# A gated mix of a long convolution and a dense layer: the signal's second stage on mirrored sums and differences, the taps loaded by pairs onto half of the partitions each

## The chip, the cores and the metric

The kernel runs on one core of a Trainium2 chip. The metric is the device time of one execution in microseconds (us), the median of several runs. The profile is one profiled execution of the same program; its times count from its first instruction.

## The reference

The input u has 2048 rows (time) of 512 channels. Two branches read it, and a gate, one number per row, mixes them. Cut to what matters:

```python
g = sigmoid((u * gate_w).sum(-1, keepdims=True))

# branch A: a state-space convolution, one filter per channel
dt = exp(log_dt)[:, None]
P = exp((dt * A)[:, :, None] * arange(L))          # A, B, C complex, [512, 128]
K = einsum("dn,dnl,dn->dl", C, P, dt * B).real     # the taps, [512, 2048]
a = irfft(rfft(pad(u.T)) * rfft(pad(K)))[:, :L].T + u * Dskip

# branch B: a dense layer, 512 -> 1792 -> 512
b = gelu(u @ w1 + b1) @ w2 + b2

return g * a + (1 - g) * b
```

## The kernel before

All work on TensorE is in float32. The kernel has two parts.

The **front part** (`front`, up to about 398 us) holds three streams of work: the dense branch (`hidden`, `output`; each operand split into a high and a low part, so that every product is three matmuls, lines 917 to 919 and 962 to 964), the taps K (powers of the poles on VectorE and ScalarE, contracted on TensorE at line 726), and the first stage of the transform of both the signal and the taps (`first_stage`, line 438). Every instruction or small group of them is a `Task` with a due time, an estimate of how long it holds its engine, and the tiles it reads and writes. `Plan.run` puts the tasks of each engine in order by due time, among those that are ready, and the instructions are then issued in that order. The due times come from formulas with the constants at the head of the file (`T_0`, `D_EV` and so on).

The transform of 2048 points (with zeros behind it, at shifted frequencies) is cut into two stages. With time as 32 x 64, the first stage transforms the 32 and leaves, for each of 32 frequencies k, 128 rows: real and imaginary parts of 64 slots. It works with products of 32 rows by 64 columns and writes its result to memory: the signal's to `tu_d[k]` (line 459), the taps' to `tk_d[k]` (line 767, eight stores of small pieces for each quarter of the channels). The 64 slots are ordered as 32 and their 32 mirror images (`slot_q`). In `signal` (line 446) a step loads two of sixteen blocks of the input (line 452), runs the first stage on both with the same matrix `c1t`, copies the four results on ScalarE (line 456) and stores them in eight pieces. `early` (line 466) brings 27 of the 32 blocks of `tu_d` back into places that have become free (`attic`, `loft`, `den`).

The **last stage** (`conv`, from about 398 us) is written out by hand. It has 16 loops s, each for two frequencies n = 2s and 2s + 1. Its steps, with the order in which they are issued in a loop:

- `fetch` (line 1129): on SyncE's queue, loads of the taps' blocks `tk_d[k]`, 256 KB on 128 partitions each, into one of eight buffers or, for n from 16 to 23, into the places of `t3`, which hold results only later. For s from 4 on, the five blocks of the signal for which there was no place are loaded as well (line 1274).
- `product(s)`: on VectorE, the complex product of the signal and the taps, six operations (lines 1174 to 1179), into the tiles v.
- `signal(s + 1)`: the second stage of the signal on TensorE, into p2u. `taps(s + 2)`: the same for the taps, into p2k, and two copies on ScalarE (line 1160). Both go through `pair` (line 1146): for the real and the imaginary part c, and for each of the two frequencies, one product of 128 rows by 64 columns. The matrix for c = 0 is f, as loaded; that for c = 1 is f1, made from f by swapping its halves with a sign (`matrices`, line 1131).
- `inverse(s)` (line 1191): the first stage back, into pa, four products of 64 rows by 64 columns.
- `turn(s)`: two copies on ScalarE (line 1197), two stores to `t4_d` (line 1199), and after every eighth frequency the loads of the transposed blocks into `den` and `t3`, mostly on GpSimd's queue.
- after every odd s up to 11, `matrices` makes f1 for the loops s + 3 and s + 4, in two copies of 64 rows on ScalarE (lines 1140 and 1141; for the first two on GpSimd, lines 1137 and 1138). The taps that use it first are those issued in loop s + 1.
- from s = 7 on, `dense` loads the dense branch's results from `out` and `gated` scales them on ScalarE.

Behind the loops, `rest` runs the last products of the dense branch (lines 1245 to 1247) while the last blocks turn, and the last stage back (line 1316) with the gate writes `out`. Before the last stage begins, the front part's last two results are added onto `out` by accumulating stores from the tiles io on GpSimd's queue (line 1006).

Of the kernel before, what the change touches and what calls it, by code (L numbers as in the profile page):

```python
# [9 lines left out]
F32 = mybir.dt.float32  # L10
# [7 lines left out]
P = 128  # L18
L = 2048
D = 512  # L20
# [13 lines left out]
T_0 = 28.031  # L34
T_MLP = 402.005
K_0 = 34.529
T_KG = 347.257
U_0 = 23
U_GAP = 18
LAG = 13.166  # L40
TABLE = 30.571
D_KA = -21.02
D_KP = -70.174
D_S1 = -64.005
D_EV = -0.687
D_H = -44.182
D_LO = -26.872
PS = (2, 3, 1, 2)
N_ACC, N_H, N_PK, N_PU = PS
D_SP = -0.459  # L50
MEM = (6, 2, 3)
N_LD, N_HL, N_ST = MEM
D_XS = -150.061
D_G = 2.936
N_WARM = 13
T_EARLY, T_LOFT, T_DEN = 434.731, 499.385, 583.061
Y_K, Y_U = 40.448, 33.741
W_MLP = (-0.0424, -0.0295, 0.0137)
W_KG = (-0.0358, -0.0266, -0.0229)
W_U = (-0.0255, -0.1355, -0.0209)  # L60
D_MAG = -1.089
D_ROT = 0.621
D_CON = -2.254
D_PHA = 0.57
D_PRE = -1.138
D_XL = 26
D_COE = -4.808
D_OUT = -10.383
D_DTB = -996.723
D_D0A = -269.982  # L70
D_LAST = -1.103
N_REST = 3
D_KA0 = 35
D_DT = 5
D_PRM = -94
D_D0 = 0
D_WAVE0 = -333.922
D_COE0 = -195.511
D_SP1 = -346.272
D_G0 = 14  # L80
D_GW = 568.694
D_XS0 = 115.71
T_PRE = 23
W_CAST = (0, 1, 0, 0, 1, 0, 1, 0, 1, 1, 0, 1, 0, 0)
X_CAST = (1, 1, 1, 1)
D_X0, D_B2, D_B2A, D_DM = -480, 20, -11.213, -79.268
N_G = 9

N_ATTIC, N_LOFT, N_TK = 11, 8, 8
# [5 lines left out]
N_US = N_DEN + N_ROOM  # L95
# [36 lines left out]
def constants():  # L132
# [14 lines left out]
    c1 = np.tile(np.stack([er, ei], 2).reshape(32, 64), (4, 1))  # L147
# [25 lines left out]
    for n, k in enumerate(ko):  # L173
# [5 lines left out]
        g2[n, :, 0, 1] = 1 - 2 * (k1 % 2)  # L179
    f2 = f2.reshape(8, 4, P, 64).transpose(0, 2, 1, 3).reshape(8, P, 256)  # L180
# [130 lines left out]
def gated_mix(  # L311
# [26 lines left out]
    tk_d = dr.tile([32, P, D], F32, name="tk_d")  # L338
# [7 lines left out]
    c1t = cp.tile([P, 64], F32, name="c1t")  # L346

    def places(attic, loft, den):
# [4 lines left out]
    def front(pool, psum, keep, attic, loft, den):  # L353
# [74 lines left out]
        def first_stage(xs, due, evac, ahead=2):  # L428
# [17 lines left out]
        def signal():  # L446
            for s in range(8):
# [3 lines left out]
                for m in range(2):  # L451
                    move(256, lambda m=m, s=s: nc.sync.dma_start(ux[m], xl[2 * s + m]), t - 10, [], [("ux", m)])
# [969 lines left out]
```

## Time and profile before

| | us |
|---|---|
| median of 3 runs (508.15 to 508.41) | 508.25 |
| profiled execution, span from first to last instruction | 506.3 |
| TensorE busy in the span | 494.8 (98%) |
| VectorE busy | 429.0 (85%) |
| ScalarE busy | 347.2 (69%) |
| GpSimd busy | 53.5 (11%) |

The profiled execution's own time is known as its span; 1.95 us lie between it and the median of the runs. In rows of the profile, PE is TensorE's matmuls and PEld its loads of matrices, DVE is VectorE, ACT ScalarE, POOL GpSimd and SP SyncE, which issues most transfers. A float32 product appears as two matmul instructions, so that `pa x8` is the four products of one `inverse`. Matmuls are pipelined: the duration of one is longer than the time from its start to the next one's, and the latter is what a product costs. The transfers of the whole span move 112.32 MB, a mean of 222 GB/s.

### The profile page before, as it was taken

The page shows a single profiled execution, that of the slowest core. Times are in us where ns is not written, and L with a number is a line of the kernel's source. Part 1 is how long each engine was busy: PE and PEld are TensorE (multiplying, and loading weights), DVE is VectorE, ACT ScalarE, POOL GpSimd, SP SyncE. Part 2 cuts the span into 40 slices and gives each one's busy share as a digit, 9 for nine tenths or more (in the row PEclk, how much of TensorE's full clock was granted, in tenths as well). Part 3 has the DMA queues.
Part 4 walks back from the last instruction along what each step waited for, and adds up shares of the span by engine and source line. Part 5 has one row for each costly group of instructions (what it writes and reads, how often), then busy time and mean ns, then how long its engine had stood idle before and what let it go on. Part 6 is the DMA issues. An engine that isn't in the chain of part 4 may idle for free.

```text
span 506.3 us, 12185 instructions
## 1 busy us (share of the span) xinstructions
PE 494.8 (98%) x4798; PEld 380.3 (75%) x4798; DVE 429.0 (85%) x794; ACT 347.2 (69%) x625; POOL 53.5 (11%) x93
## 2 busy tenths in 40 slices
PE   7999999999999999999999999999999999999995
PEld 7886988998889889889789878989889722222551
DVE  6999999998999999999899989999921188877544
ACT  4898757699683889968487997657643445568513
POOL 1001010101002011011110012001010300020003
PEclk9999999999999999999999999999999999999998
DMA  8958896416788545889850276984588997999998
GB/s 288 381 178 235 298 296 219 84 65 200 182 239 222 156 147 126 262 187 238 201 128 2 84 167 156 208 266 104 189 208 180 282 390 266 336 374 382 320 321 312
DMA packets 82680, 112.32 MB, mean 222 GB/s; under 512 B 39644, under 2 KB 41184, under 8 KB 82080
## 3 DMA queue, kind: packets, MB, share of 16 engines
q1 hardware_dynamic: 74704, 87.06, 53.7%
q0 software_dynamic: 7264, 21.73, 18.3%
q10 hardware_dynamic: 656, 2.75, 1.7%
q8 instruction: 38, 0.62, 0.5%
q14 instruction: 18, 0.15, 0.1%
HBM read 61.71 MB, written 49.81 MB: 220 GB/s over the span
## 4 chain that ended last, share of the span: by engine, by line
PE 70%; DVE 13%; DMA 7%; ACT 4%; SPq 2%; issue 2%; DVEq 0%; ACTq 0%
PE pk L726 10%; PE acc L962 7%; PE ph L917 7%; PE ph L919 7%; PE ph L918 7%; PE acc L964 7%; PE acc L963 6%; PE p2u L1152 5%; PE p2k L1152 4%; PE pa L1191 3%; PE pb L1316 3%; DMA tk<-tk_d 2%; PE ph L438 2%; DVE y L689 2%; SPq L767 2%
## 5 line engine op out<-in xcount | busy, mean ns | idle before, releaser
L917 PE MATMUL ph<-xh,wh 128*128 128x256 f32 x448 | 127.7, 285 | 2.2 <-ACT wh L826 1.6
L919 PE MATMUL ph<-xh,wl 128*128 128x256 f32 x448 | 127.1, 284 | 0.4 <-DVE wl L828 0.4
L918 PE MATMUL ph<-xlo,wh 128*128 128x256 f32 x448 | 126.7, 283 | 0.0
L917 PEld LDWEIGHTS ph<-xh,wh 128*128 128x128 f32 x448 | 85.2, 190 | 9.5 <-issue 5.0
L918 PEld LDWEIGHTS ph<-xlo,wh 128*128 128x128 f32 x448 | 85.1, 190 | 1.8
L919 PEld LDWEIGHTS ph<-xh,wl 128*128 128x128 f32 x448 | 85.1, 190 | 1.0 <-DVE wl L828 1.0
L962 PE MATMUL acc<-wh,hh 128*128 128x512 f32 x206 | 83.2, 404 | 0.1
L964 PE MATMUL acc<-wh,hl 128*128 128x512 f32 x206 | 80.9, 393 | 0.5 <-DVE hl L947 0.5
L963 PE MATMUL acc<-wl,hh 128*128 128x512 f32 x206 | 80.9, 393 | 0.0
L934 ACT ACTIVATE ph<-ph,b1t 128x256 f32<-128x256 f32 x112 | 50.4, 450 | 43.6 <-PE ph L919 41.8
L726 PE MATMUL pk<-y,den 128*32 128x64 f32 x2048 | 61.4, 290 | 0.0
L726 PEld LDWEIGHTS pk<-y,den 128*32 128x32 f32 x2048 | 57.2, 136 | 3.5 <-issue 1.4
L962 PEld LDWEIGHTS acc<-wh,hh 128*128 128x128 f32 x206 | 38.7, 188 | 17.8 <-issue 7.4
L947 DVE TENSOR_TENSOR hl<-ph,hh 128x512 fp32r<-128x512 f32 (+1 forms) x62 | 38.4, 620 | 14.9 <-ACT hh L937 14.6
L689 DVE TENSOR_TENSOR y<-y,ea 128x64 f32<-128x64 f32 (+4 forms) x80 | 45.5, 569 | 2.1 <-ACT y L679 1.5
L964 PEld LDWEIGHTS acc<-wh,hl 128*128 128x128 f32 x206 | 38.7, 188 | 10.3 <-DVE hl L947 1.7
L963 PEld LDWEIGHTS acc<-wl,hh 128*128 128x128 f32 x206 | 38.7, 188 | 6.2
L937 ACT CAST hh<-ph 128x512 fp32r<-128x512 f32 (+1 forms) x62 | 33.0, 533 | 9.4 <-PE acc L963 6.2
L532 DVE TENSOR_TENSOR loft<-den,zz 128x256 f32<-128x256 f32 (+2 forms) x48 | 37.4, 779 | 0.7
L533 DVE TENSOR_TENSOR loft<-den,zz 128x256 f32<-128x256 f32 (+2 forms) x48 | 37.3, 777 | 0.0
L701 DVE TENSOR_TENSOR y<-y,loft 128x2048 f32<-128x2048 f32 x16 | 36.6, 2288 | 0.6 <-ACT loft L650 0.5
L1160 ACT COPY k<-p2k 128x512 f32<-128x512 f32 x32 | 18.5, 585 | 23.8 <-PE p2k L1152 8.0
(190 smaller groups left out, 876.0 us busy)
## 6 DMA issues: line engine op xcount, KB each, us to landing
tu_d<-attic SPq DMA_DIRECT2D x64, 128.0 KB, 3.9
tk_d<-sk SPq DMA_DIRECT2D x32, 256.0 KB, 5.3
t_d<-sa SPq DMA_DIRECT2D x32, 256.0 KB, 5.4
tk<-tk_d SPq DMA_DIRECT2D x24, 256.0 KB, 5.1
attic<-in_xt_dram SPq DMA_DIRECT2D x16, 256.0 KB, 5.1
xh_d<-xh SPq DMA_DIRECT2D x8, 512.0 KB, 5.0
xl_d<-xlo SPq DMA_DIRECT2D x8, 512.0 KB, 4.6
attic<-in_xs_dram SPq DMA_DIRECT2D x16, 256.0 KB, 4.9
```

Of the source, the lines that this page charges most:

```text
L532: vec(2 * m, lambda: vv.tensor_mul(t, a, br), due, [ka, *kb], [kt])
L689: nc.vector.tensor_mul(both(n, 64 - 3 * n, n), both(0, 64 - n, n), an)
L726: nc.tensor.matmul(pks[q][32 * j : 32 * j + 32, :, gg], x[:, r, :, ch], y[:, r, :, ch], start=(r == 0), stop=(r == 1), skip_group_check=True,)
L917: nc.tensor.matmul(p, h, xh[xk][:, d], start=(d == 0), stop=False)
L918: nc.tensor.matmul(p, h, xlo[xk][:, d], start=False, stop=False)
L919: nc.tensor.matmul(p, lo, xh[xk][:, d], start=False, stop=(d == 3))
L934: nc.scalar.activation(phs[q][:, n], phs[q][:, n], AF.Gelu_apprx_tanh, bias=b1t[:, f : f + 1])
L947: nc.vector.tensor_sub(lo, phs[q][:, 0:nf], hi.bitcast(F32))
L962: nc.tensor.matmul(a, h, wh[1][w], start=start, stop=False)
L963: nc.tensor.matmul(a, h, wl[1][w], start=False, stop=False)
L964: nc.tensor.matmul(a, l, wh[1][w], start=False, stop=(j == 3))
L1152: nc.tensor.matmul(out[64 * i : 64 * i + 64], w, x, start=True, stop=True)
```

## The change

**The signal.** A step of `signal` now takes block s and its mirror image, block 8 + s. It loads one into each buffer, negates the second on ScalarE, and adds the other block onto each with an accumulating load on GpSimd's queue, so that the buffers hold the sum and the difference. The first stage runs on both, on the difference with the real and imaginary columns of the matrix swapped. The 64 rows of each part of `tu_d[k]` are then 32 of sums and 32 of differences, and in the second stage the real part needs only the first 64 rows and the imaginary part only the last 64: each product has 64 rows in place of 128, and f alone, without f1.

**The taps.** `tk_d` is split in two halves of the slots, and `fetch` brings the blocks of a pair of frequencies into one tile, with one load for partitions 0 to 63 and one for 64 to 127. The order of the rows of f follows, and `matrices` makes f1 in four pieces of 32 rows in place of two of 64. The eight buffers of one block become five of two.

**Places.** Five more places (`shed`) let `early` bring all 32 blocks of the signal, so the five loads in the last stage go.

**Order.** Every task of the front part gets a due time from a list `DUE`, and the constants at the head are changed. The scratch space for descriptors of GpSimd's transfers is set to 2048.

```diff
-T_0 = 28.031
-T_MLP = 402.005
+T_0 = 30.181
+T_MLP = 394.707
...
+D_UL, D_UN, D_UA = -26.734, -19.978, -26.418
...
-N_ATTIC, N_LOFT, N_TK = 11, 8, 8
+N_ATTIC, N_LOFT, N_TK = 11, 8, 5
...
-N_US = N_DEN + N_ROOM
+
+DUE = (
+    -14012, -3058, -1619, -990, 254, -1062, 252, 2164, -206, -437, -438, -558, -1021, -1047, -3081, -2791, -3683,
...
+)
...
-    c1 = np.tile(np.stack([er, ei], 2).reshape(32, 64), (4, 1))
+    c1 = np.concatenate([np.stack(z, 2).reshape(32, 64) for z in ((er, ei), (ei, er))], 1)
+    c1 = np.tile(c1, (4, 1))
...
+    f2 = f2.reshape(32, 2, 2, 32, 64).transpose(0, 2, 1, 3, 4)
     f2 = f2.reshape(8, 4, P, 64).transpose(0, 2, 1, 3).reshape(8, P, 256)
...
-    tk_d = dr.tile([32, P, D], F32, name="tk_d")
+    tk_d = dr.tile([2, 32, 64, D], F32, name="tk_d")
...
-        return [den[:, k] for k in range(N_DEN)] + rooms + rooms[: 32 - N_US]
+        return [den[:, k] for k in range(N_DEN)] + rooms + [shed[:, k] for k in range(32 - N_DEN - N_ROOM)]
...
-                        nc.tensor.matmul(bank[64 * m : 64 * m + 64], c1t[rs], x[rs], start=True, stop=True)
+                        w = c1t[rs, 64 * m * mirrored : 64 * m * mirrored + 64]
+                        nc.tensor.matmul(bank[64 * m : 64 * m + 64], w, x[rs], start=True, stop=True)
...
                 for m in range(2):
-                    move(256, lambda m=m, s=s: nc.sync.dma_start(ux[m], xl[2 * s + m]), t - 10, [], [("ux", m)])
+                    move(256, lambda m=m, s=s: nc.sync.dma_start(ux[m], xl[8 * m + s]), t + D_UL, [], [("ux", m)])
+                act(512, lambda: nc.scalar.mul(ux[1], ux[1], -1.0), t + D_UN, [], [("ux", 1)])
+                for m in range(2):
+                    move(
+                        540, lambda m=m, s=s: nc.gpsimd.dma_start(ux[m], xl[8 * (1 - m) + s], accum_op=ALU.add),
+                        t + D_UA, [], [("ux", m)], queue="GP", hold=0.8,
+                    )
...
-                            128, lambda m=m: nc.sync.dma_start(rows[:, 8 * s + 4 * m + r], st[k][64 * m : 64 * m + 64]),
-                            t, [("st", k)], [("u_d", 8 * s + 4 * m + r)], out=True,
+                            128, lambda m=m: nc.sync.dma_start(rows[:, 32 * m + 4 * s + r], st[k][64 * m : 64 * m + 64]),
+                            t, [("st", k)], [("u_d", 32 * m + 4 * s + r)], out=True,
...
-                first_stage(xs, t, evac)
+                first_stage(xs, t, evac, mirrored=1)
...
-            for n in range(N_US):
+            for n in range(32):
...
+                sr = slice(h // 2 % 2 * 16, h // 2 % 2 * 16 + 16)
...
-                        tk_d[:, :, d : d + 64].rearrange("k (c s) g -> (k c) s g", c=2)[:, ss],
+                        tk_d[h // 4, :, :, d : d + 64].rearrange("k (c s) g -> (k c) s g", c=2)[:, sr],
...
+        for t, due in zip(pl.tasks, DUE, strict=True):
+            t.due = due / 10
         for t in pl.run():
             t.fn()
...
-        def fetch(n):
-            if 16 <= n < 24:
-                t2s[n] = t3[:, n]
+        def fetch(s):
+
+            n = 2 * s
+            if 8 <= s < 12:
+                t = t3[:, n : n + 2]
             else:
-                t2s[n] = pool.tile([P, D], F32, tag="tk", name=f"tk{n}", bufs=N_TK)
-            nc.sync.dma_start(t2s[n], tk_d[ko[n]])
+                t = pool.tile([P, 2, D], F32, tag="tk", name=f"tk{s}", bufs=N_TK)
+            t2s[n], t2s[n + 1] = t[:, 0], t[:, 1]
+            for h in range(2):
+                rows = tk_d[h].rearrange("(a b) q d -> b q a d", b=8)[ko[n] % 8][:, ko[n] // 8 : ko[n] // 8 + 2]
+                nc.sync.dma_start(t[64 * h : 64 * h + 64], rows)
...
-            if m < 2:
-                nc.gpsimd.tensor_scalar(f1[0:64], f[64:128], -1.0, None, ALU.mult)
-                nc.gpsimd.tensor_copy(f1[64:128], f[0:64])
-            else:
-                nc.scalar.mul(f1[0:64], f[64:128], -1.0)
-                nc.scalar.copy(f1[64:128], f[0:64])
+            for a in (0, 64):
+                re, im = slice(a, a + 32), slice(a + 32, a + 64)
+                if m < 2:
+                    nc.gpsimd.tensor_scalar(f1[re], f[im], -1.0, None, ALU.mult)
+                    nc.gpsimd.tensor_copy(f1[im], f[re])
+                else:
+                    nc.scalar.mul(f1[re], f[im], -1.0)
+                    nc.scalar.copy(f1[im], f[re])
...
-                w = mats[n // 4][0][c][:, n % 4]
-                x = t2s[n] if r else us[n]
+                if r:
+                    w, x = mats[n // 4][0][c][:, n % 4], t2s[n]
+                else:
+                    h = slice(64 * c, 64 * c + 64)
+                    w, x = mats[n // 4][0][0][h, n % 4], us[n][h]
                 nc.tensor.matmul(out[64 * i : 64 * i + 64], w, x, start=True, stop=True)
...
-            for n in range(2 * s + N_ROOM, min(2 * s + N_ROOM + 2, 32)) if s > 3 else ():
-                nc.sync.dma_start(us[n], tu_d[ko[n]])
...
+    shed = keep.tile([P, 32 - N_DEN - N_ROOM, D], F32, name="shed")
...
-    nc = bacc.Bacc("TRN2", target_bir_lowering=False, num_devices=1)
+    nc = bacc.Bacc("TRN2", target_bir_lowering=False, num_devices=1, dynamic_dma_scratch_size=2048)
```

More of the change, by code (lines that the diff above doesn't have):

```diff
@@ L33 @@
 NB = 2 * NSB
-T_0 = 28.031
-T_MLP = 402.005
[L36 to L47, printed above, removed]
+T_0 = 30.181
+T_MLP = 394.707
+K_0 = 37.105
+T_KG = 355.412
+U_0 = 22.335
+U_GAP = 18.311
+LAG = 13.918
+TABLE = 32.374
+D_KA = -25.837
+D_KP = -7.351
+D_S1 = -39.706
+D_EV = -4.468
+D_H = -49.631
+D_LO = -47.233
 PS = (2, 3, 1, 2)
 N_ACC, N_H, N_PK, N_PU = PS
-D_SP = -0.459
+D_SP = 6.17
+D_UL, D_UN, D_UA = -26.734, -19.978, -26.418
 MEM = (6, 2, 3)
 N_LD, N_HL, N_ST = MEM
-D_XS = -150.061
+D_XS = -73.683
 D_G = 2.936
 N_WARM = 13
[L56 to L61, printed above, removed]
-D_ROT = 0.621
[L63 to L71, printed above, removed]
-N_REST = 3
[L73 to L84, printed above, removed]
+T_EARLY, T_LOFT, T_DEN = 268.769, 88.647, 688.804
+Y_K, Y_U = 39.373, 32.963
+W_MLP = (-0.0402, -0.0382, 0.0137)
+W_KG = (-0.0552, -0.0303, -0.0248)
+W_U = (-0.0299, -0.1355, -0.0182)
+D_MAG = -1.108
+D_ROT = 0.621
+D_CON = -2.853
+D_PHA = 0.521
+D_PRE = -0.43
+D_XL = -21.252
+D_COE = -12.806
+D_OUT = -43.76
+D_DTB = -1371.399
+D_D0A = -89.28
+D_LAST = 3.23
+N_REST = 3
+D_KA0 = 66.334
+D_DT = 3.379
+D_PRM = -94.216
+D_D0 = 19.524
+D_WAVE0 = -640.267
+D_COE0 = -98.47
+D_SP1 = -328.657
+D_G0 = -7.172
+D_GW = 807.205
+D_XS0 = 238.814
+T_PRE = 62.946
+W_CAST = (0, 0, 0, 1, 1, 0, 1, 0, 0, 1, 0, 1, 0, 0)
 X_CAST = (1, 1, 1, 1)
-D_X0, D_B2, D_B2A, D_DM = -480, 20, -11.213, -79.268
+D_X0, D_B2, D_B2A, D_DM = -252.638, 6.525, -2.867, 78.983
 N_G = 9
-N_ATTIC, N_LOFT, N_TK = 11, 8, 8
+N_ATTIC, N_LOFT, N_TK = 11, 8, 5
 ASIDE = (4, 6, 13, 14)
@@ L345, in gated_mix, with places, front @@
     gate = cp.tile([P, 2, 16], F32, name="gate")
-    c1t = cp.tile([P, 64], F32, name="c1t")
-    def places(attic, loft, den):
+    c1t = cp.tile([P, 128], F32, name="c1t")
+    def places(attic, loft, den, shed):
         rooms = [attic[:, k] for k in range(N_ATTIC)] + [loft[:, k * D : k * D + D] for k in range(N_LOFT)]
-        return [den[:, k] for k in range(N_DEN)] + rooms + rooms[: 32 - N_US]
-    def front(pool, psum, keep, attic, loft, den):
+        return [den[:, k] for k in range(N_DEN)] + rooms + [shed[:, k] for k in range(32 - N_DEN - N_ROOM)]
+    def front(pool, psum, keep, attic, loft, den, shed):
         pl = Plan()
@@ L426, in front, with first_stage @@
         step = [0]
-        def first_stage(xs, due, evac, ahead=2):
+        def first_stage(xs, due, evac, ahead=2, mirrored=0):
             q = (step[0] + ahead) % N_H
@@ L1107, in front, with conv @@
         return sorted(late, key=lambda e: e[0])
-    def conv(pool, ps, late, attic, loft, den):
+    def conv(pool, ps, late, attic, loft, den, shed):
         sas = [pool.tile([P, D], F32, name=f"sa{k}", bufs=1) for k in range(6)]
         zs = [pool.tile([P, D], F32, name=f"z{k}", bufs=1) for k in range(2)]
-        us = places(attic, loft, den)
+        us = places(attic, loft, den, shed)
         ko = k0_order()
@@ L1349, in gated_mix @@
     ):
-        late = front(kp, ps, keep, attic, loft, den)
+        late = front(kp, ps, keep, attic, loft, den, shed)
     with (
@@ L1354, in gated_mix @@
     ):
-        conv(fp, ps_f, late, attic, loft, den)
+        conv(fp, ps_f, late, attic, loft, den, shed)
 _NAMES = [
```

20 lines of the change are left out of this document (10 added, 10 removed), and 87 rows, old and new, of the table DUE.

## The prediction

> **What bounds the kernel now.** I read the page first, then the busy time by stretch, then the chain of work that ended last, then the timeline of one loop of the last stage, then the transfers.
>
> ```profile
> PE 494.8 (98%) x4798; PEld 380.3 (75%) x4798; DVE 429.0 (85%) x794; ACT 347.2 (69%) x625; POOL 53.5 (11%) x93
> PE 70%; DVE 13%; DMA 7%; ACT 4%; SPq 2%; issue 2%; DVEq 0%; ACTq 0%
> ```
>
> TensorE is busy for 98% of the span and holds 70% of the chain. The average hides stages, so the next view cuts the span into stretches (us; then for each engine busy us and instructions; granted clock, DMA share, GB/s).
>
> ```profile
> 0.00:20.00 20.00, 17.00 (x110) 15.74 (x111) 15.66 (x39) 11.50 (x24) 2.08 (x10) 1.00 0.90 322
> 20.00:60.00 40.00, 38.35 (x262) 32.62 (x261) 38.90 (x90) 37.12 (x67) 2.95 (x4) 1.00 0.78 249
> 60.00:240.00 180.00, 180.00 (x2116) 157.30 (x2118) 175.10 (x329) 140.80 (x254) 17.34 (x30) 1.00 0.69 189
> 240.00:300.00 60.00, 59.42 (x736) 50.53 (x728) 57.00 (x108) 46.22 (x83) 7.40 (x14) 1.00 0.48 120
> 300.00:398.00 98.00, 98.00 (x1085) 86.61 (x1084) 70.25 (x117) 57.10 (x101) 11.13 (x19) 1.00 0.74 189
> 434.00:472.00 38.00, 38.00 (x200) 10.43 (x196) 29.90 (x49) 25.98 (x49) 3.67 (x7) 1.00 1.01 375
> 394.00:506.00 112.00, 106.00 (x542) 41.53 (x541) 72.75 (x116) 56.98 (x104) 14.78 (x21) 0.99 0.95 333
> ```
>
> The planned front part (up to about 398 us) leaves TensorE idle for only 3.00 + 1.65 + 0.58 = 5.2 us, most of that at the start. From 394 us the transfers are busy for 95% of the time, and for all of it between 434 and 472 us: whatever shortens the last stage pushes against that.
>
> The chain (start, us, what) shows what a loop of the last stage costs: pa is the inverse, p2u the signal's second stage, p2k the taps'.
>
> ```profile
> 408.91 1.69 PE pa L1191 x8
> ...
> 414.18 1.02 PE pa L1191 x8
> ...
> 432.59 1.02 PE pa L1191 x8
> 433.61 1.87 PE p2u L1152 x8
> 435.48 1.72 PE p2k L1152 x8
> 437.19 1.02 PE pa L1191 x8
> ...
> 469.42 1.02 PE pa L1191 x8
> ...
> 475.60 1.02 PE pa L1191 x8
> ```
>
> One loop takes 437.19 - 432.59 = 4.60 us and is TensorE from end to end. The inverses run from 408.91 (loop 0) over 414.18 (loop 1) and 469.42 (loop 13) to 475.60 us (loop 15).
>
> **The change, part by part.** *The signal's products.* The timeline of one loop (start, duration, engine, line; in brackets what the engine waited for):
>
> ```profile
> 432.52 1.09 PE L1191 MATMUL pa<-v,cc 64*64 64x512 f32 x8
> 433.54 1.08 PE L1152 MATMUL p2u<-attic,cc 128*64 128x512 f32 x4
> 433.67 1.07 ACT L1197 COPY sa<-pa 128x512 f32<-128x512 f32 x2 [0.37 <-PE pa L1191]
> 434.45 1.03 PE L1152 MATMUL p2u<-attic,f 128*64 128x512 f32 x4
> 434.77 0.41 ACT L1140 ACTIVATE f<-cc 64x256 f32<-64x256 f32 x1
> 435.19 0.40 ACT L1141 COPY f<-cc 64x256 f32<-64x256 f32 x1
> 435.31 1.03 PE L1152 MATMUL p2k<-t,cc 128*64 128x512 f32 x4
> 435.74 0.14 PEld L1152 LDWEIGHTS p2k<-t,f 128*64 128x64 f32 x2 [0.29 <-ACT f L1141]
> 436.16 1.03 PE L1152 MATMUL p2k<-t,f 128*64 128x512 f32 x4
> 437.12 1.09 PE L1191 MATMUL pa<-v,cc 64*64 64x512 f32 x8
> ```
>
> From start to start: pa 1.02, p2u 0.91 and 0.86, p2k 0.85 and 0.96 us, together 4.60. A p2u block is two products of 128 rows, one per half of the output columns. After the change each product has 64 rows, and the four of a loop fall on four different quarters of the array, as the four of pa do now; pa does its four in 1.02 us. So p2u's 0.91 + 0.86 = 1.77 us become one block: at least 0.86 (a block with no change of shape near it), at most pa's 1.02. I take 0.91, because pa and p2u would now have one shape and the change of shape moves behind p2u, to p2k, without a new one. The loop then needs 4.60 - 1.77 + 0.91 = 3.74 us of TensorE (3.69 to 3.85).
>
> The Trainium skill's page TensorEngine Tiling (Array Packing), section Key Properties, says that a change of tiling mode drains the array. The trace agrees: the blocks that stand at a change of shape are the long ones (1.02, 0.91 and 0.96 against 0.86); by that rule alone the block is 0.86 and the loop 3.69 us.
>
> *Is VectorE next?* In loop 0, behind the wait at L1175, it ran without a break:
>
> ```profile
> 403.72 0.69 DVE L1174 TENSOR_TENSOR v<-p2u,k 128x512 f32<-128x512 f32 x1 [4.05 <-ACT k L1160]
> 406.37 0.69 DVE L1175 TENSOR_TENSOR v<-p2u,k 128x512 f32<-128x512 f32 x1 [1.95 <-DMA out_dram<-io]
> ...
> 409.37 0.69 DVE L1174 TENSOR_TENSOR v<-p2u,k 128x512 f32<-128x512 f32 x1
> ```
>
> L1175 to the next L1174 are five operations in 3.00 us: 0.60 each, so the six of a loop make 3.60 us, just under 3.74. VectorE doesn't bind, by 0.14 us.
>
> *The matrices f1: the wait that replaces what is saved.* ScalarE now makes f1 in two copies of 64 rows; after the change in four of 32 rows, each with the same 256 elements per row, so 0.42 and 0.40 us twice. They stand on ScalarE behind the copies of pa, and the taps of the very next loop need them for their second block. Now they are done at 435.59 and the block starts at 436.16, so nothing is lost. After the change they are done 0.82 us later, 3.89 us after the start of the inverse; with the 0.15 us to the weight load and its 0.14, the block starts at 4.18. TensorE would be there at 1.02 + 0.91 + 0.86 = 2.79. So TensorE waits 1.39 us in each loop that follows matrices: behind loops 1, 3, 5, 7, 9 and 11. Such a pair of loops takes 4.18 + 0.96 + 3.74 = 8.88 us against 9.20 now: 0.32 us saved instead of 1.72. Queued behind the copies on ScalarE are the next two copies of p2k; TensorE needs their banks only a loop later, so they cost nothing more. Six pairs from loop 1 to loop 13: **-1.9 us**. For m 0 and 1 GpSimd makes the four pieces, twice as long as now; there the first products wait for a transfer until 406.37 us, which covers it: 0.
>
> *Loop 0 and its start.* The first product waits for the two accumulating stores out_dram<-io: L1175 starts when the second has landed. That is a wait for memory: v[1] lies where io lay. The tap tiles grow from 8 x 2 to 5 x 4 KB per partition, which by the order of the allocations moves v by 4 KB, so that L1174 falls on that same wait. It then starts at 406.37 and one more operation stands behind it: +0.6 us (bounds: +0.6; or -2.0, the L1175 wait, if no tile lies there any more). From loop 0 to loop 1 the 5.27 us lose p2u's 0.86: together **-0.3 us**.
>
> *Loops 13 to 15* take 6.18 us. There are no taps any more, and TensorE will run into VectorE: the product of loop 14 begins some 1.5 us ahead of the inverse of loop 13 (the taps' 0.86 + 0.96 lie between, less the way from engine to engine), two products take 7.2 us, and 0.3 lead back to TensorE: 6.0 us, **-0.2 us**. Behind that, the tail (the outputs held back, the last stage, the stores) is unchanged and shifts as a whole: 0.
>
> *The signal's first stage* (front part). Eight more negations on ScalarE and sixteen accumulating transfers on GpSimd's queue; the products keep their number, and only their matrices differ. The nearest rows:
>
> ```profile
> L456 ACT COPY attic<-pu 128x512 f32<-128x512 f32 x16 | 9.6, 598 | 6.9 <-DMA tu_d<-attic 6.8
> out_dram<-b2b POOLq DMA_DIRECT2D x16, 256.0 KB, 5.9
> xh<-xh_d POOLq DMA_DIRECT2D x8, 512.0 KB, 4.2
> ```
>
> Eight times 0.6 us is 4.8 us on an engine that is idle for over a fifth of the front part, and 5.9 us more from load to product, eight times in 300 us. Behind the transfers on GpSimd's queue stand the reloads of xh, which TensorE does need. I cost it at 0, as the plan places it early; were the cover gone, TensorE would wait some 6 us a step.
>
> *The new order of the front part* (a due time for each task) issues the same products. It can win at most the idle time behind the first 20 us, 1.65 + 0.58 = 2.2 us; for a loss the nearest row is a reload of xh that comes late by its whole 4.2 us. I take 0, and -2.2 to +4.2 for the range.
>
> *The rows of the taps.* The same 32 x 256 KB, but each load on 64 partitions, and five loads of the signal move from the last stage to the front part. What a transfer on 64 partitions costs is seen at the stores of the signal's first stage, when they run alone, beside transfers on all partitions:
>
> ```profile
> 250.00:250.40 0.40, 0.40 (x4) 0.32 (x3) 0.40 (x1) 0.04 (x1) 0.00 (x0) 1.00 1.00 215
> 410.00:414.00 4.00, 4.00 (x22) 1.06 (x16) 4.00 (x8) 1.64 (x3) 0.00 (x0) 1.00 1.05 388
> ```
>
> Fully busy engines carry 215 GB/s on one half and 388 on all. So a load of 0.67 us could take up to 1.22. Between 394 and 506 us the engines work 0.95 x 112 = 106.4 us; five loads fewer make 103.0. The forecast's end (503.9) leaves 109.9 - 1.6 (the end, where the last stores trickle) = 108.3, so the loads may cost 5.3 us more, 0.16 each, before they set the end. With other transfers and the other half queued beside them I expect them under that: two halves in flight at once would carry twice 215.
>
> **Sum.** -1.9 - 0.3 - 0.2 = -2.4 us: span 506.3 to 503.9. The median of the runs is 508.25, so 1.95 us lie around the span, which I leave: **505.9 us**.
>
> **The rivals.** *ScalarE's copies don't hold TensorE* (say that they shrink with the rows): then each of the 12 loops gains 0.86, 10.3 us in place of 1.9: 508.25 - 10.3 - 0.3 - 0.2 = 497.4. Against it: a copy of 64 rows already takes 0.40. Chance 0.10.
>
> *The half-partition loads set the end* (slower). One mechanism: engines that meet on one half carry 215 GB/s. From 0.16 us more per load it eats the gain, from 0.23 us (7.4 us in all) the kernel is slower than now; at the full 0.55 it is 103.0 + 17.6 = 120.6 us from 394 on, a span of 514.6 and a time of 516.5. For it: the 215 row, and a last stage already at 0.95. Against it: the taps run five pairs ahead. Chance 0.14, a part of it mild. The Trainium skill, SBUF — State Buffer, section "Can I just issue two DMAs to hit both halves?", says no: two halves serialize. By it the full price is paid, 516.5. The 215 row agrees for a half alone; no row here shows two loads into both halves.
>
> *The front part moves*, by its new order or by the accumulating transfers: 0.08 faster (505.9 - 2.2 = 503.7), 0.08 slower (505.9 + 4.2 = 510.1).
>
> *It cancels*: a little from the loads, a little from the start, within 0.2% (1 us, which is about what a measurement of this kernel can tell from none): chance 0.12.
>
> The forecast itself, faster by 1 to 5 us, has 0.48. **Chances:** faster 0.48 + 0.10 + 0.08 = 0.66; same 0.12; slower 0.14 + 0.08 = 0.22. **Range:** 498.5 to 510.5; it leaves out the first rival (0.10) and the full price of the second (some 0.10).
>
> **What would show it.** Right: in the chain p2u x8 at about 0.9 us; in every second loop ScalarE's f1 as releaser of the weight load of p2k, over 1 us; inverses of a pair 8.9 us apart, single ones 3.7; L1174 of loop 0 waiting for out_dram<-io. Wrong: p2k or pa waiting for tk<-tk_d (the loads), pairs 7.5 us apart (no wait for f1), p2u x8 still at 1.7 (the quarters don't run together), or a last stage that starts more than 2 us off 398 (the order).

## The result and the profile after

The changed kernel takes 522.13 us (median of 4 runs, 521.45 to 523.92) against 508.2 for the kernel before: a ratio of 1.0285 [1.025, 1.032]. It is slower by 14 us, outside the range given. The profiled execution has a span of 519.3 us, 13.0 more than before. Where the median and the ratio of a run below don't match, some of its executions took longer at a lower granted clock; the ratio leaves these out.

The first lines of the page, of the changed kernel (busy time by engine; shares of the chain that ended last):

```profile
PE 489.5 (94%) x4798; PEld 376.5 (73%) x4798; DVE 429.9 (83%) x793; ACT 357.8 (69%) x647; POOL 70.1 (14%) x113
PE 67%; DMA 15%; issue 5%; ACT 4%; SPq 4%; DVE 3%; POOL 1%; ACTq 1%; DVEq 0%; POOLq 0%
```

TensorE is busy for 5.3 us less, in a span that is 13.0 longer; transfers hold 15% of the chain where they held 7%. The stretches of the changed kernel (us; busy us and instructions of PE, PEld, DVE, ACT, POOL; granted clock, DMA share, GB/s):

```profile
20.00:60.00 40.00, 36.82 (x253) 31.30 (x251) 37.56 (x87) 32.98 (x59) 5.00 (x7) 1.00 0.87 249
60.00:240.00 180.00, 177.45 (x2003) 153.45 (x1996) 174.06 (x327) 144.36 (x260) 24.52 (x38) 1.00 0.74 200
406.00:410.00 4.00, 0.00 (x0) 0.00 (x0) 0.04 (x1) 0.00 (x0) 1.04 (x2) 0.65 1.09 265
414.00:430.00 16.00, 14.99 (x94) 3.81 (x96) 14.47 (x24) 9.22 (x18) 0.27 (x1) 1.00 1.06 230
```

In the front part TensorE idles 3.18 us from 20 to 60 us (1.65 before) and 2.55 from 60 to 240 (none before), and the clock granted in the first 20 us is 0.91: from 8 to 12 us it is 0.59, by which these 4 us lose some 1.6 (an estimate). Against the kernel before that makes some 5 of the 6.4 us that the front part ends later. The rest was not found. Between 406 and 410 us TensorE does nothing at all. From 414 to 430 us the transfer engines are busy throughout and carry 230 GB/s.

Four rows of the timeline cut the span into parts. Of the kernel before: the last product of the front part, the first of the taps, the inverses of loops 0 and 15.

```profile
398.03 0.28 PE L919 MATMUL ph<-xh,wl 128*128 128x256 f32 x1
398.24 0.64 PE L1152 MATMUL p2k<-tk,cc 128*64 128x512 f32 x1
408.91 0.64 PE L1191 MATMUL pa<-v,cc 64*64 64x512 f32 x1 [0.93 <-DVE v L1178]
475.53 0.66 PE L1191 MATMUL pa<-v,cc 64*64 64x512 f32 x4
```

The same four of the changed kernel:

```profile
404.39 0.28 PE L1020 MATMUL ph<-xh,wl 128*128 128x256 f32 x1
410.66 1.12 PE L1265 MATMUL p2k<-tk,cc 128*64 128x512 f32 x2 [5.99 <-DMA tk<-tk_d]
419.96 0.66 PE L1304 MATMUL pa<-v,cc 64*64 64x512 f32 x4
486.89 0.64 PE L1304 MATMUL pa<-v,cc 64*64 64x512 f32 x1
```

| part of the span, us | before | after | difference |
|---|---|---|---|
| to the last product of the front part | 398.0 | 404.4 | +6.4 |
| from there to the first product of the taps | 0.2 | 6.3 | +6.1 |
| to the inverse of loop 0 | 10.7 | 9.3 | -1.4 |
| to the inverse of loop 15 | 66.6 | 66.9 | +0.3 |
| to the end | 30.8 | 32.4 | +1.6 |

So the time is lost ahead of the last stage (6.4), at its start (6.1), and inside it, where nothing is gained although its loops have less to do. The chain of the changed kernel shows why the last two go together (L1251 is a copy of `matrices`):

```profile
402.78 9.94 DMA tk<-tk_d
412.74 8.29 DMA tk<-tk_d
421.04 8.40 DMA t<-tk_d
429.51 7.03 DMA t_d<-sa
...
438.49 0.41 ACT f L1251
438.95 1.98 PE p2k L1265 x4
```

For 34 us the end hangs on tap loads, one behind the other in SyncE's queue, and then on a store of the inverse's result that stands behind them. ScalarE can't copy the next result until that store has landed, f1 stands behind that copy, and the taps' second block behind f1. Beyond 451 us the loops run free, and there they look as forecast:

```profile
451.50 1.02 PE pa L1304 x8
452.53 0.86 PE p2u L1265 x8
453.38 1.87 PE p2k L1265 x8
455.25 1.02 PE pa L1304 x8
...
459.15 1.08 PE p2k L1265 x4
460.23 1.02 PE pa L1304 x8
```

A single loop takes 3.75 us (451.50 to 455.25), the loop behind matrices 4.98, a pair 8.73.

### The profile page after: what moved, and what is told of

The parts are those of the page before. It is cut to its first block, busy times and chain, and to the rows that moved or that the text cites. A ratio compares the mean times of both kernels' runs of the same rounds, so it can differ in the third digit from the quotient of the medians.

```text
span 519.3 us, 12259 instructions
## 1 busy us (share of the span) xinstructions
PE 489.5 (94%) x4798; PEld 376.5 (73%) x4798; DVE 429.9 (83%) x793; ACT 357.8 (69%) x647; POOL 70.1 (14%) x113
## 4 chain that ended last, share of the span: by engine, by line
PE 67%; DMA 15%; issue 5%; ACT 4%; SPq 4%; DVE 3%; POOL 1%; ACTq 1%; DVEq 0%; POOLq 0%
PE pk L826 10%; PE ph L1018 8%; PE ph L1019 8%; PE acc L1063 8%; PE ph L1020 8%; PE acc L1064 7%; PE acc L1065 7%; DMA ux<-in_xl_dram 4%; DMA tk<-tk_d 4%; PE p2k L1265 3%; PE ph L532 3%; PE pa L1304 2%; DMA t_d<-sa 2%; SPq L868 2%; PE p2u L1265 2%
## 5 line engine op out<-in xcount | busy, mean ns | idle before, releaser
L1018 PE MATMUL ph<-xh,wh 128*128 128x256 f32 x448 | 129.1, 288 | 3.5 <-ACT wh L927 2.9
L826 PE MATMUL pk<-y,den 128*32 128x64 f32 x2048 | 61.6, 291 | 0.8 <-DVE y L812 0.8
```

Source lines behind the costliest of these rows:

```text
L826: nc.tensor.matmul(pks[q][32 * j : 32 * j + 32, :, gg], x[:, r, :, ch], y[:, r, :, ch], start=(r == 0), stop=(r == 1), skip_group_check=True,)
L1018: nc.tensor.matmul(p, h, xh[xk][:, d], start=(d == 0), stop=False)
```

## The experiments

The theory after the result: three independent costs, the halves of the taps, the four pieces of f1, and the front part; the rivals are named with each run. Each kernel was timed beside the kernel before on the same chip; the kernel before had medians from 506.6 to 508.2 there, so ratios are compared rather than times of different calls.

### The loads by themselves: m1_loads_alone

Behind the end of the kernel before, six groups of loads of tk_d, one after another.

```diff
+        done()
+        for load in (
+            whole, lambda: alternating((nc.sync, nc.sync)), one_half, every_second,
+            lambda: alternating((nc.sync, nc.scalar)), whole,
+        ):
+            load()
+            done()
```

> The kernel before, with loads from tk_d into t3 added behind its end, in six groups that wait for one another: 12 whole loads of 256 KB; 12 of 256 KB on partitions 0-63 and 64-127 in turn, as the change has them; 12 of 128 KB on partitions 0-63 alone; 12 of 256 KB on every second partition; the halves in turn again, one half from SyncE's queue and the other from ScalarE's; 12 whole ones again. Theory (two halves in one queue run one behind the other, each at half the rate): 0.67 us a load whole, 1.14 for the halves in turn (as the changed kernel's trace has them), 0.57 for the 128 KB, 0.67 for every second partition. Rival (the loads were slow because of what ran beside them): 0.67 in all groups of 256 KB.

Three stretches: whole loads, halves in turn from one queue, loads of every second partition.

```profile
504.00:512.00 8.00, 0.00 (x0) 0.00 (x0) 0.00 (x0) 0.00 (x0) 0.00 (x0) 0.50 1.00 358
520.00:528.00 8.00, 0.00 (x0) 0.00 (x0) 0.00 (x0) 0.00 (x0) 0.00 (x0) 0.50 1.07 225
548.00:552.00 4.00, 0.00 (x0) 0.00 (x0) 0.00 (x0) 0.00 (x0) 0.00 (x0) 0.50 1.02 373
```

The last two columns decide: the engines are equally busy, and with halves they carry 225 GB/s against 358 and 373. Whole loads land mostly 0.64 to 0.68 us apart, halves of the same 256 KB 1.13 to 1.19, so a load costs some 0.5 us more, with nothing else in flight. The Trainium skill, SBUF — State Buffer, section "Can I just issue two DMAs to hit both halves?", says that two such transfers serialize; the 225 agrees, the 334 of e4 below doesn't. Every second partition at the full rate shows that it is the half that costs, not the 64 partitions. Halves issued in turn from two queues landed 0.97 us apart on average (0.55 to 1.74), so that a part of the loss stays. The loads of 128 KB on one half landed 0.67 us apart (0.57 was expected), about as fast as they were issued, one every 0.64 us.

### The taps whole again: e1_whole_taps

```diff
-            for h in range(2):
-                rows = tk_d[h].rearrange("(a b) q d -> b q a d", b=8)[ko[n] % 8][:, ko[n] // 8 : ko[n] // 8 + 2]
-                nc.sync.dma_start(t[64 * h : 64 * h + 64], rows)
+            for i in range(2):
+                nc.sync.dma_start(t[:, i], tk_d[ko[n + i]])
```

The signal gets a copy of f in its own row order, in wider constants.

> The changed kernel with the taps stored and loaded as before, on all 128 partitions (two loads of 256 KB per pair, four tiles of two in place of five); the signal's products get a copy of the matrix in their own order of rows, 1 MB more of constants in all; f1 stays in four pieces, the order of the front part stays. Theory (the half loads cost what lies behind the front part's end): the front part ends at 404.5 us as in the changed kernel, the first inverse comes 10.7 us later (415.2, in place of 420.0), and loops 0 to 13 take some 57 us in place of 61.5: span near 509, time near 511. Rival (the loads are hidden, the front part and cold clocks make the rest): at least 518.

515.44 us, ratio 1.0152 [1.0118, 1.0187]: 6.7 us below the changed kernel, half of the loss. Its front part and the start of its last stage:

```profile
403.47 0.28 PE L1020 MATMUL ph<-xh,wl 128*128 128x256 f32 x1
408.52 1.08 PE L1265 MATMUL p2k<-tk,cc 128*64 128x512 f32 x1 [4.77 <-DMA tk<-tk_d]
418.67 0.66 PE L1304 MATMUL pa<-v,cc 64*64 64x512 f32 x4
480.28 0.64 PE L1304 MATMUL pa<-v,cc 64*64 64x512 f32 x1
```

Loop 0 to 15 takes 61.6 us in place of 66.9, so 5.3 of the 6.7 lay in the loops: in the changed kernel the inverses at 432.42 and 446.46, a pair of loops, lie 14.0 us apart, in e1 every such pair 8.7. The front part and the 5 us to the first taps stay: these are not the halves. The theory had expected the start of the last stage to come back as well, and so a time near 511.

### The order of before: e2_old_order and e3_whole_old_order

Both drop the list `DUE` and take the constants of the kernel before; e3 has whole taps as well, so that only the signal's part of the change is left.

> The changed kernel with the constants at its head as before and without the list of due times; the three new constants of the signal's loads stay. Half loads stay. Theory (the new order costs the front part its 6.3 us): the front part ends at 398 to 400 us again and the time is 516 to 518. Rival (the accumulating loads and the negations cost it): the front part still ends at 403 to 406 and the time stays at 521 to 524.

> The changed kernel with the front part in the order of the kernel before (its constants, no list of due times) and the taps loaded whole, 256 KB on 128 partitions each: of the change, only the signal is left (sums and differences by accumulating loads, half-height products, all 32 blocks fetched early, f1 in four pieces). Theory (the accumulating loads delay TensorE in the front part, whatever the order): the front part's last product is as late as with the old order and half loads (406.9, against 398.0 before), the loops run at 3.75 and 4.98, and the time is about 515. Rival (the half loads were what made the front part late in the old order too): last front product at 398 to 400, time 505 to 507.

e2 takes 516.69 us (1.0184 [1.0156, 1.0211]), e3 513.39 (1.0115 [1.0088, 1.0142]). Of e3:

```profile
404.99 0.28 PE L929 MATMUL ph<-xh,wl 128*128 128x256 f32 x1
405.20 0.64 PE L1172 MATMUL p2k<-tk,cc 128*64 128x512 f32 x1
```

In e2 the front part ends at 406.97: the time that its theory named was met, the reason for it was not. Two things follow. The front part is as late in the order of the kernel before, so the signal's part brings it along; and the wait at the start of the last stage is gone, so that one belongs to the new order. The traces point at how. The two accumulating stores of io and the first tap loads, in the changed kernel, then in e3:

```profile
399.03 1.72 POOL L1107 DMA_DIRECT2D out_dram<-io  x2 [1.10 <-ACT io L1084]
400.62 0.61 SPq L1237 DMA_DIRECT2D tk<-tk_d  x1
```

```profile
399.04 0.84 SPq L1143 DMA_DIRECT2D tk<-tk_d  x2
402.84 1.72 POOL L1016 DMA_DIRECT2D out_dram<-io  x2
```

Issued behind the stores, the first load took 9.1 us to land in the changed kernel, 8.6 in e1 and 7.3 in e15 (below), and landed 0.2 to 0.5 us after the second store; issued ahead of them, it took 4.3 us in the kernel before, 5.6 in e3 and 4.5 in e17. No run moved these two stores alone, so their part is argued from the traces. The halves cost 3.3 us in this order (e2 against e3).

### The halves in the kernel before: e4_halves_alone and e11_halves_old_layout

e4 is the kernel before with the pair loads by halves out of the undivided tk_d; e11 is e1 with the same loads.

```diff
+            rows = tk_d.rearrange("(a b) q d -> b q a d", b=8)[ko[n] % 8][:, ko[n] // 8 : ko[n] // 8 + 2]
+            for h in (slice(0, 64), slice(64, 128)):
+                nc.sync.dma_start(t[h], rows[h])
```

> The kernel before, with the rows of the taps loaded by pairs onto half of the partitions each (256 KB, the same bytes and number of loads, four tiles of two in place of eight of one); nothing else of the change. Theory (half loads run at half the rate and hold the start of the last stage): the first inverse comes 6 to 10 us later than 408.9 and none of it is won back, so 514 to 518. Rival (the loads are hidden behind the loops): 508 to 509.

> The kernel of e1_whole_taps with the taps loaded by pairs onto half of the partitions each, but out of the undivided tk_d of the kernel before, as in e4_halves_alone: it differs from the changed kernel in where the rows lie in memory, not in which partitions they go to. Theory (two halves in turn move at the rate of one, wherever they come from): landings 1.1 us apart between 412 and 430, packets of 2 KB at about 150 ns, time 520 to 523, as the changed kernel. Rival (the divided layout is what makes the halves slow, and out of the undivided one they overlap, as the 0.8 us and 102 ns of e4_halves_alone hint): landings 0.8 apart, time 516 to 518.

e4 took only 508.79 us, ratio 1.0045 [1.0025, 1.0066]: the price named for it was missed. A stretch of e4:

```profile
412.00:420.00 8.00, 8.00 (x46) 2.12 (x44) 7.41 (x13) 5.03 (x10) 0.00 (x0) 1.00 1.05 334
```

The engines carry 334 GB/s here, a packet of 2 KB takes 102 ns on average, and the loads land about 0.8 us apart; in the changed kernel it is 230 GB/s, 149 ns and 1.14 us. So in this run halves did overlap in part. e11 has e4's layout and the changed kernel's order, and its loads are 1.05 apart; it takes 519.89 us (1.0237 [1.0186, 1.0288]), 0.85% more than e1 by the ratios. So the halves are slow out of e4's layout too. What decides whether two halves overlap, the phase in which the engines meet or what else is in flight, stays open.

### What costs in the front part: e5, e8, e9, e10, e6

Five runs take the signal's first stage apart; the code is cut to the calls that change. e5: the second loads without the accumulation. e8: negations and second loads left out, all else at its place. e9: no change but one due time in the kernel before. e10: sixteen more loads, which nobody waits for, in the kernel before, with the change's scratch space for descriptors. e6: sums on GpSimd.

```diff
e5  -  nc.gpsimd.dma_start(ux[m], xl[8 * (1 - m) + s], accum_op=ALU.add)
    +  nc.gpsimd.dma_start(ux[m], xl[8 * (1 - m) + s])
e8  -  nc.scalar.mul(ux[1], ux[1], -1.0)
    +  None
    -  nc.gpsimd.dma_start(ux[m], xl[8 * (1 - m) + s], accum_op=ALU.add)
    +  None
e9  -  nc.sync.dma_start(ux[m], xl[2 * s + m]), t - 10,
    +  nc.sync.dma_start(ux[m], xl[2 * s + m]), t - 26.734,
e10 +  nc.gpsimd.dma_start(shed[:, 2 * (s % 2) + m], xl[2 * s + m])
e6  +  nc.gpsimd.tensor_add(ux[0], ux[0], ux[1])
    +  nc.scalar.mul(ux[1], ux[1], -2.0)
    +  nc.gpsimd.tensor_add(ux[1], ux[1], ux[0])
```

> The kernel of e3_whole_old_order with the sixteen accumulating loads of the signal made plain loads of the same blocks, same queue, same tasks, same order. Left out: the sums and differences, so the signal's transform is of wrong data. Theory (what costs is the accumulation itself, whose packets take 176 ns per 2 KB against 84): the front part's last product comes back to 399 to 401 and the time to about 508. Rival (what costs is the longer chain of load, negation, second load, product and the place of these steps in ScalarE's and GpSimd's order): last front product within 2 us of that of e3_whole_old_order, time within 2 us of it.

> The kernel of e3_whole_old_order with the eight negations and the sixteen second loads of the signal left out, while every other step stays at its place in the order of every engine. Left out: the sums and differences, so the signal's transform is of wrong data. Theory (TensorE waits because a step of the signal now has three steps more in a row, load, negation, second load, before its product): the front part's last product comes back from 404.9 to 398 to 400 us, and the time from 513.4 to about 507. Rival (it is the order of the other steps, which the added ones have upset, not the added work): last front product at 403 to 406, time at 512 to 514.

> The kernel before with one constant of the order changed: the signal's loads are due 26.734 us ahead of their step, as in the changed kernel, in place of 10. No work is added. Theory (the front part's order is so finely set that a step moved for no other reason costs several us): last front product at 402 to 406 against 398.0, time 512 to 515. Rival (the order holds such a shift): last front product within 1 us of 398, time within 1 us of the kernel before.

> The kernel before with sixteen more loads of the signal's blocks, issued on GpSimd's queue right behind the loads that stand there, into places that nobody reads, and with the scratch space for descriptors of GpSimd's transfers at 2048 as in the change. The order of everything else is as before. Theory (4 MB more of transfers in the front part, a half of it in its first 100 us, where the transfer engines are busy for 61 to 94%, delays the loads that TensorE waits for): last front product at 400 to 402, time 510 to 512. Rival (the bytes cost nothing, the chain or the order does): last front product within 0.7 us of 398.0, time within 1 us of the kernel before.

> The kernel of e3_whole_old_order with the sums and differences made on GpSimd: both blocks loaded plainly as before, a sum in place (1.27 us for 128x512 in the profile), ScalarE's multiplication by -2, a second sum in place. No accumulating loads for the signal. Theory (the accumulating loads make the front part late): last front product at 399 to 401, time about 508. Rival (the longer chain and its place in the order do, whatever makes the sums): last front product over 404, time over 512.

The last product of the front part in e8, then in e9, each from its timeline:

```profile
403.89 0.28 PE L929 MATMUL ph<-xh,wl 128*128 128x256 f32 x1
```

```profile
402.64 0.28 PE L919 MATMUL ph<-xh,wl 128*128 128x256 f32 x1
```

Against the 398.03 of the kernel before, and with the same row of the other runs:

| run | time, us | ratio | front part against before |
|---|---|---|---|
| e3, the signal's part | 513.39 | 1.0115 [1.0088, 1.0142] | +7.0 |
| e5, no accumulation | 513.08 | 1.0111 [1.0081, 1.0141] | +7.4 |
| e8, added steps left out | 511.84 | 1.0097 [1.0061, 1.0133] | +5.9 |
| e9, one due time, no added work | 512.49 | 1.0122 [1.0092, 1.0151] | +4.6 |
| e10, 16 loads, old order | 510.07 | 1.0065 [1.0040, 1.0091] | +1.3 |
| e6, sums on GpSimd | 523.38 | 1.0309 [1.0275, 1.0343] | +18.2 |

The accumulation costs nothing that shows (e5). Leaving the added steps out altogether wins only 1.1 us of 7.0 back (e8), less than runs with one and the same front part differ by (it ends at 404.99 in e3, 405.40 in e7, 406.61 in e12). And the kernel before loses 4.6 us of the front part and 1.2% of its time to a due time moved by 17 us, with no work added (e9). My theory that the longer way from load to product holds TensorE falls: what costs is that the order of the other steps has been upset. The extra loads have a price too, 0.65% of the time (e10); their 1.3 us of the front part lie inside that spread. Why the sums on GpSimd cost as much as 18 us (e6) was not taken apart: they are other work in another order. Where most of the loss happens can be read in e3. TensorE and ScalarE near 50 us:

```profile
50.11 0.49 PE L972 MATMUL acc<-wh,hh 128*128 128x512 f32 x1 [3.73 <-ACT hh L947]
```

```profile
45.51 1.18 ACT L659 ACTIVATE loft<-loft,half_pi 128x1056 f32<-128x1056 f32 x1
46.57 0.63 ACT L456 ACTIVATE ux<-ux 128x512 f32<-128x512 f32 x1
47.22 1.28 ACT L944 ACT_TABLE_LOAD   x1
48.51 0.93 ACT L944 ACTIVATE ph<-ph,b1t 128x256 f32<-128x256 f32 x2
```

And ScalarE in the kernel before:

```profile
43.22 0.59 ACT L937 CAST hh<-ph 128x512 fp32r<-128x512 f32 x1
...
44.82 1.28 ACT L649 ACT_TABLE_LOAD   x1
```

Before, ScalarE makes the dense branch's hh first and then loads the table for the sines. In e3 the sines come first; hh, which TensorE needs next, stands behind them, the negation and a table load, and TensorE waits 3.73 us. In e9, where nothing was added, the sines (the last at 45.23 us) and a table load (46.42) have moved ahead of hh (48.67) as well:

```profile
49.31 0.79 PE L962 MATMUL acc<-wh,hh 128*128 128x512 f32 x1 [2.92 <-ACT hh L937]
```

Behind these waits the granted clock was 0.65 from 52 to 56 us in e3 and 0.62 from 48 to 52 in e9, by that share another 1.4 and 1.5 us (estimates). So the wait and the clock behind it come to 5.1 us in e3 and 4.4 in e9, against losses of 7.0 and 4.6; other waits grew and shrank beside them. In the changed kernel, whose order is another, the wait for hh at this place is 1.64 us.

### The wait for f1: e7_two_pieces and e12_matrices_earlier

e7 is e3 with f1 in two copies of 64 rows; e12 issues them one loop earlier (the cut is e12's).

```diff
-            if s % 2 and s < 13:
+            if s % 2 == 0 and s < 12:
                 matrices(s // 2 + 2)
```

> The kernel of e3_whole_old_order with f1 made in two copies of 64 rows, as in the kernel before (the whole layout of the taps allows it). Theory (the four pieces hold TensorE in every second loop): the wait of 1.24 us behind matrices shrinks by the two copies that go, 0.82, to about 0.4; pairs of loops at 7.9 in place of 8.73; six pairs, 4.9 us less than e3_whole_old_order. Rival (another wait takes its place, VectorE's six operations of 0.6 us or ScalarE's copies): pairs above 8.3, less than 2.5 us.

> The kernel of e7_two_pieces with matrices issued one loop earlier (after every even s up to 10, so that ScalarE has a loop more for f1). Theory (the 0.40 us that TensorE still waits in every second loop are the wait for f1): pairs of loops at 7.49 in place of 7.88, six pairs, 2.3 us off the loops; the end of the kernel takes a part back, since the transfers there set the pace already in e7_two_pieces (the last stage back starts 2.5 us behind the last product ahead of it): time 508 to 509. Rival (VectorE's 3.60 per loop or ScalarE's copies hold the loops as well): pairs stay at 7.8 or more, time as e7_two_pieces, 509.3.

e7: 509.27 us, ratio 1.0037 [1.0016, 1.0057]. e12: 507.66, ratio 1.0001 [0.9985, 1.0016]. Inverses in the chain of e7, then of e12:

```profile
421.30 1.02 PE pa L1209 x8
...
425.44 1.02 PE pa L1209 x8
...
429.18 1.02 PE pa L1209 x8
```

```profile
422.96 1.02 PE pa L1209 x8
...
426.71 1.02 PE pa L1209 x8
...
430.45 1.02 PE pa L1209 x8
```

Pairs take 7.88 us, then 7.49: every loop at 3.74 or 3.75, and the wait for f1 is gone. VectorE's 3.60 per loop does not bind, up to loop 13. But the end gives some back: from the inverse of loop 15 to the end e12 takes 32.8 us, before 30.8, and its last stage back opens with a wait for a transfer, which there was not before:

```profile
487.88 0.65 PE L1332 MATMUL pb<-den,g1t 128*64 128x512 f32 x2 [2.00 <-DMA den<-t_d]
```

### Other orders of the same work: e13, e14, e15, e16, e17

e13, e14 and e16 are e12 with three lists of due times of my own. e15 is the changed kernel with its own list, whole taps and the two mends of f1. e17 is e15 with a list that leaves slack for late transfers and keeps the taps' last stores and first loads ahead of the front part's end.

```diff
+DUE = (
...
+)
...
+        for t, due in zip(pl.tasks, DUE, strict=True):
+            t.due = due / 10
         for t in pl.run():
             t.fn()
```

> The kernel of e12_matrices_earlier with a list of due times for the front part's tasks, set for these tasks (with the accumulating loads among them) and so that the taps' stores and first loads stay ahead of the front part's end. The same work. Theory (of the 6 to 7 us that the front part loses, most is order and can be won back): last front product at 401 to 403 against 405.3, first tap product within 0.5 us of it, time 3 us below e12_matrices_earlier, 504 to 506. Rival (the added steps cost this whatever the order, as even the changed kernel's list of its own leaves 403.5 to 404.4): last front product at 404 or later, time within 1.5 us of e12_matrices_earlier.

> As e13_new_order, with another list of due times, of the same making. What two orders of the same work differ by shows how far the order alone moves the front part's end. Theory (order): both end the front part ahead of 404, and they differ by 1 us or more. Rival (added work): both at 404 or later.

> The changed kernel with its own order of the front part, and the two faults of its last stage mended: the taps loaded whole, f1 in two copies of 64 rows and issued a loop earlier. Theory (what is left is the front part, 403.5 at its end, and the start of the last stage, 5 us behind it, since the accumulating stores of io are issued ahead of the first taps): last front product at 403 to 404, first tap product 4 to 6 us later, loops at 3.74, time 508.5 to 511. Rival (with the loads whole and the loops short the start comes back by itself): first tap product within 1 us of the last front product, time 504 to 506.

> The kernel of e12_matrices_earlier with a third list of due times, chosen so that the order still holds when transfers land late by a random delay of 0.6 us on average (the lists of e13_new_order and e14_other_order were not). Theory (orders that fit the estimates too closely lose on the chip; with slack the front part ends earlier): last front product at 402 to 405 against 406.6, time 504 to 506. Rival (the added steps cost it in any order): last front product over 405.5, time within 1 us of e12_matrices_earlier, 507.7.

> The kernel of e15_mended with a list of due times made with the same slack, from the changed kernel's own list, and with the taps' last stores kept 5.5 us ahead of the front part's end. Theory (as for e16_slack_order, and the start of the last stage is mended as well): last front product at 401 to 404, first tap product within 1.5 us of it, time 503 to 506. Rival (in any order): over 404, time 507 or more.

| run | time, us | ratio | last front product, us |
|---|---|---|---|
| e13 | 511.89 | 1.0079 [1.0051, 1.0108] | 410.22 |
| e14 | 516.23 | 1.0128 [1.0084, 1.0173] | 413.88, in an execution of 519.04 us |
| e15 | 509.0 | 1.0011 [0.9978, 1.0045] | 404.93 |
| e16 | 507.98 | 1.0008 [0.9976, 1.0040] | 404.66 |
| e17 | 501.52 | 0.9885 [0.9848, 0.9921] | 399.92 |

e13 missed what its theory expected, and so did e14: the two lists made without slack gave the slowest of these kernels. e16 is level with e12, against its theory. e17 shows what the order alone can be worth. The work is that of e15, the order is another, and its four executions (500.31 to 502.68) all lie below the ten of e15 (504.35 to 513.94):

```profile
399.92 0.28 PE L1010 MATMUL ph<-xh,wl 128*128 128x256 f32 x1
400.75 1.52 PE L1253 MATMUL p2k<-tk,cc 128*64 128x512 f32 x3 [0.55 <-ACT ph L1025]
```

The front part ends within 1.9 us of the kernel before, the first taps come 0.8 us behind it (their loads go out at 396.15, the stores of io at 396.94), and the kernel is faster than the kernel before, by 1.15%, and than the changed one, by 4%. Why this list holds on the chip and that of e16 doesn't is not shown. Its last stage, in the stretches:

```profile
394.00:498.00 104.00, 95.40 (x553) 37.89 (x551) 72.52 (x116) 57.63 (x106) 14.65 (x20) 0.99 1.00 361
```

The transfer engines are busy for all of it, so I expect nothing more from a faster loop there; no run tried it.

## Why the prediction was wrong, point by point

*The second stage of the signal: right.* In the chain p2u is 0.86 us and the loop 3.75 (3.74 forecast). From start to start, as the forecast counted, p2u is 0.96 (0.91 forecast) and pa 0.91 (1.02), with the same sum. In the chain the 0.15 us for the change of shape have moved from p2u (1.87 before) to the taps (1.72 before, 1.87 now). The 3.69 that the prediction drew from the Trainium skill, TensorEngine Tiling (Array Packing), section Key Properties, was not reached.

*VectorE: right.* It never bound where there are taps; e12 and e17 run these loops at 3.74 or 3.75.

*f1 in four pieces: right in mechanism, a little too dear.* 1.39 us were forecast for a loop behind matrices, 1.23 (4.98 - 3.75) were measured. A pair takes 8.73, forecast 8.88. Mending it was worth 4.1 us in e7 and a further 0.36% in e12 (by the ratios, some 1.8 us).

*Loop 0, its start and loops 13 to 15: too small.* The product of loop 0 did not wait for out_dram<-io; the late taps covered that. In e17, where the taps are early again, it waits for it, 3.96 us. With whole taps (e1) loops 0 to 15 win 5.0 us, where the sum had 3.0 for them: loop 0 wins 1.45 (0.86 forecast), the six pairs 2.9 (1.9), loops 13 to 15 0.6 (0.2).

*The rows of the taps: wrong, and the first step that failed.* "With other transfers and the other half queued beside them I expect them under that: two halves in flight at once would carry twice 215." They carry 225 alone and 230 in the changed kernel: 0.47 us more per load, three times the 0.16 at which the loads were to set the end. Against e1 it cost 6.7 us; with the layout of before (e11) the halves alone cost 0.85%, some 4.3 us. The row of 215 GB/s stood in the prediction and gave nearly the right price; I argued it away on a supposition of which no row spoke, and gave the rival that used it 0.14. The rival's full price, 10.6 us over the forecast, was too high by 3.9; and in e4, where the halves overlapped in part, they cost 0.45%.

*The new order and the signal's first stage: wrong, the second step that failed.* "I cost it at 0, as the plan places it early", with -2.2 to +4.2 us for the order. It was +6.4, and it did not come from what the bounds had been made of, a late reload of xh, but, as far as it was traced, from steps of a full plan that changed places: there one moved due time costs 4.6 (e9), and sixteen more loads alone cost 0.65% of the time (e10). In the changed kernel itself the 6.4 is spread over several short waits and a slow clock, and which step of its list brought them is not shown. e17 shows the other side: with all the added work, another order leaves +1.9.

*The start of the last stage: missing from the sum.* 6.1 us. The sign was named ("p2k or pa waiting for tk<-tk_d"), but only as a result of the halves; 4.8 of it comes with whole taps too (e1), and none in the old order (e3). The traces put it on two accumulating stores issued ahead of the first loads, which no run moved alone.

*The tail at 0: wrong in size.* +1.6 us, which was not taken apart. Where the loops are shorter (e12), the last stage back waits 2.00 us for a transfer, and 2.0 us of the gain went there.

## What to carry to other kernels

A transfer onto half of the partitions moved at 0.6 of the rate of a whole one here, with the other half queued right behind it; price it by its own row until a run shows an overlap. When steps are added to a part that is ordered by a full plan and keeps TensorE busy nearly throughout, a price of nothing is the one that needs a reason: the order itself is a cost, and another order of the same work was worth some 7 us (e15 to e17). A gain in one stage of a kernel whose transfers are already at 95% there should be followed to the last store before it is counted.

## What the runs showed of the hardware that was not expected

- TensorE came back slowly from its waits: at 406 to 410 us, idle, its granted clock was 0.65, and the taps' block at 438.95, behind a wait of 3.57 us, took 1.98 us (granted clock 0.50 from 438 to 442) where the same block at 459.15 took 1.08. A stall costs more than its own length. The Trainium skill, TensorE: Matmul & The Clock Gate, section Part 1: The HAM clock gate, says that an array without work falls back to half of its clock and needs to be busy for a while; the trace agrees.
- An accumulating load of 256 KB into on-chip memory landed 7.0 us after its issue in e3 (median), a plain one from the same queue 5.3 in e5. The time did not show it: the ratios are 1.0115 and 1.0111, each inside the other's interval.
